# Threshold attention and a gated feed-forward block: operands laid out on the host, query tiles of two heads, float32 values in two column halves

## The chip, the cores and the metric

The program runs on one core of a Trainium2 chip. The metric is the device time of one execution in microseconds (us), lower is better. The kernel before took 1152.54 us, the median of 3 runs (1152.47 to 1153.68).

A core has a tensor engine (PE), which multiplies a stationary operand (loaded first, shown as PEld) with a moving one and writes to PSUM, and the engines DVE (vector), ACT (scalar) and POOL (GpSimd), which work on SBUF; DVE and ACT also read PSUM. SP issues the DMAs here.

## The reference, cut to what matters

```python
# q, k, v: (8 batches, 8 heads, 576 tokens, 64), float32; tau = 0.02
scores = matmul(q, k.transpose(0, 1, 3, 2)) / 8
thresh = max(scores, -1) - tau
scores = where(scores >= thresh, scores, -1e9)
attn = exp(scores - max(scores, -1))
attn = attn / (sum(attn, -1) + 1e-9)
x = matmul(attn, v)                       # then the heads side by side: (8, 576, 512)
x_prev = x one token earlier, zeros first
xk = mu_k * x + (1 - mu_k) * x_prev
xr = mu_r * x + (1 - mu_r) * x_prev
k = maximum(xk @ w_k, 0)                  # 512 -> 1024
out = sigmoid(xr @ w_r) * ((k * k) @ w_v) # 1024 -> 512
```

The weights w_k, w_r and w_v come as float64 words and are cut to float32 on the chip.

## The kernel before

**Precision.** A matmul whose operands are marked fp32r keeps fewer bits of them than float32. So most products are made of an upper part (the rounded value) and a lower part (what the rounding left): upper by upper, upper by lower, lower by upper. A matmul on plain float32 needs no split; in the trace each one is two MATMUL records with a weight load each.

**Attention.** A *job* is one batch and two heads (`hp`), 32 in all. Its 576 queries per head are cut into four tiles of 128 per head and one tile "T" that holds the last 64 queries of both heads, so nine tiles. Each tile is one *slot*, 288 in all; `full` (L633) is the order in a job. A tile goes through `scores` (L297; four matmuls of 288 columns, eight for T, through the zero-padded stationary `bd`), `row_max` (DVE, L338), `threshold` (ACT, L342), `expo` (ACT, L346), `mask` (DVE, L351), `denom` and `inverse` (DVE, L355, L358), `norm` (POOL, L361), `turn_p` (five PE transposes into `pt`, L368), `p_hi` (ACT, L393, upper part), `p_lo` (DVE, L403, lower part) and, for two tiles of a head together, `attend` (nine matmuls, L439) and `attend_out` (ACT L447, DVE L449, L456). The scores' PSUM tiles `ps_s` have two buffers, one for each of two slots.

**Operands of a job.** `load` and `load_v` fetch q, k and v with tokens on the partitions; `prep_steps` turns q and k with nine PE transposes (L189), splits them (L206 to L225), copies the parts with eight DMAs from SBUF to SBUF so that upper and lower part lie on the two halves of the partitions (`stack`, L231), fills `bd` on POOL (L249) and splits v (L277, L278). The plans `PREP` and `PREP0` (L739) spread that over the slots of the job before.

**While the tensor engine has nothing else to do.** Job 0 (`whole`) makes its scores in plain float32 (L308) on 64 partitions, and jobs 0 to 4 (`plain`) make probabilities by values in plain float32 (L412).

**Feed-forward.** 18 chunks of 256 tokens, each of 20 PE steps: eight `h` steps (twelve matmuls of 256 columns), four `z` and eight `vps` steps (six matmuls of 512 columns), all at L525. POOL and ACT mix x with x_prev and split it (L485 to L510), ACT and DVE make relu and square (L551, L554), ACT and POOL split them (L557, L558), DVE multiplies by the gate (L616), and DMAs store the rows. `weight_steps` (L119) turns one of 20 weight pieces (128 rows, 512 columns) into float32 parts, a piece every two slots: ACT (L128), DVE (L132, then L136 to L138), ACT (L142), POOL (L146). Its scratch is `xT[1]`, which later holds x of the odd batches.

**The order.** `slot(n)` (L784) issues the work of a slot, with each tile's stages spread over five slots. A credit in planned PE time decides how many feed-forward steps a slot gets: a slot adds `TSLOT` 3.325, its planned PE time is taken off, each step takes `TSTEP` 1.3, and `KEEP` 10 steps are held back until the last chunk is there. A chunk can be used from four slots after its last tile. Only ACT works strictly in this written order (L72); for the other engines a planner orders what is ready at build time, earlier lines first.

Of the kernel before, what the change touches and what calls it, by code (L numbers as in the profile page):

```python
# [15 lines left out]
# float32 readings of the upper words of the doubles 2**-127 and just under 2**128  # L16
# [5 lines left out]
def tile_threshold_attention_then_rwkv_ffn(  # L22
    ctx: ExitStack,
    tc: tile.TileContext,
    q: bass.AP,
    k: bass.AP,
    v: bass.AP,
    tau: bass.AP,
    mu_k: bass.AP,
    mu_r: bass.AP,  # L30
# [8 lines left out]
    B, H, S, D = q.shape  # L39
    DM, DF = w_k.shape  # L40
    P = 128
    NPAIR = H // 2
    NCT = DM // P
# [3 lines left out]
    NC4 = SM // P  # L47
    HS = S // 2
    KT = S
    KM = S + ST  # L50
    W = 2 * S
# [18 lines left out]
    ps_t = ctx.enter_context(tc.tile_pool(name="ps_t", bufs=1, space=bass.MemoryType.PSUM))  # L70
# [6 lines left out]
    # The threshold uses max(tau, 0).  A negative tau masks every key, which leaves  # L77
    # equal scores, so the queries are scaled by zero then.
# [9 lines left out]
    # x^T of the first 512 tokens of a batch, behind a column of what comes before  # L88
    # them (zeros), and of the last 64 tokens, behind a copy of token 511.
# [7 lines left out]
    vraw = const.tile([P, 2, 5 * D], F32, name="vraw")  # L97

    # stationaries of the scores' tile that holds both heads' last 64 queries
# [3 lines left out]
    # The weights come as float64 words.  Each is cut to float32 (saturating, with what  # L103
    # lies under float32's normal range flushed to zero): the sign and the top bit of
    # the exponent stay, the three exponent bits under it repeat it in that range, and
    # the rest moves up by three bits.
    # A piece (128 rows, 512 columns) becomes its upper and lower part, where its words lay.
    pieces = {}

    def weight_jobs():  # L110
        jobs = []
        for nm, w in (("k", w_k), ("r", w_r), ("v", w_v)):
            for f in range(w.shape[1] // 512):
                for c in range(w.shape[0] // P):
                    src = w[c * P : (c + 1) * P, f * 512 : (f + 1) * 512]
                    jobs.append(((nm, c, f), src))
        return jobs

    def weight_steps(j, key, src):  # L119
# [3 lines left out]
        w1, w0 = words[:, :, 1], words[:, :, 0]  # L123
        box = {}

        def s1():
            box["t"] = xT[1][:, j % 4 if j < 16 else 1 + (j - 16) % 3, 1 : 1 + 512]
# [23 lines left out]
    def load(job):  # L151
        b, hp = job["b"], job["hp"]
        hs = slice(2 * hp, 2 * hp + 2)
        raw = p1.tile([P, 9, 2, D], F32, tag="raw", name="raw")
        job["raw"] = raw
        for h in range(2):
            for g in range(2):
                SY.dma_start(
                    raw[:, 2 * g : 2 * g + 2, h],
                    q[b, 2 * hp + h, 2 * g * P : 2 * (g + 1) * P, :].rearrange("(p c) d -> p c d", c=2),  # L160
                )
            SY.dma_start(
                raw[:, 4:8, h], k[b, 2 * hp + h, 0:SM, :].rearrange("(p c) d -> p c d", c=NC4)
            )
        for s, src in ((0, q), (1, k)):
            SY.dma_start(
                raw[D * s : D * s + D, 8], src[b, hs, SM:S, :].rearrange("h s d -> s h d")
            )

    def load_v(job):  # L170
        b, hp = job["b"], job["hp"]
        hs = slice(2 * hp, 2 * hp + 2)
        SY.dma_start(
            vraw[:, :, 0 : 4 * D],
            v[b, hs, 0:SM, :].rearrange("h (p c) d -> p h (c d)", c=NC4),
        )
        for y in range(2):
            SY.dma_start(
                vraw[y * D : (y + 1) * D, :, 4 * D :], v[b, hs, SM:S, :].rearrange("h s d -> s h d")
            )  # L180

    def prep_steps(job):
        raw = job["raw"]
        box = {}

        def turn(nm, idx):
            ps = ps_w.tile([P, 512], F32, tag="w", name=nm)
            for j, i in enumerate(idx):
                PE.transpose(ps[:, j * P : (j + 1) * P], raw[:, i].rearrange("p h d -> p (h d)"), ident)  # L189
            box[nm] = ps  # L190

        def q_turn():
            if job["whole"]:
                job["qk"] = p3.tile([P, W], F32, tag="st1", name="qk")
                turn("pq", range(4))
                return
            box["hi"] = p1.tile([P, W], FR, tag="hi", name="hi")
            box["lo"] = p1.tile([P, W], FR, tag="lo", name="lo")
            turn("pq", range(4))

        def evac_q(cols, ps):
            if job["whole"]:
                A.activation(job["qk"][:, cols], ps, AF.Copy, scale=qscale)
                return
            hi, lo = box["hi"][:, cols], box["lo"][:, cols]
            A.activation(hi, ps, AF.Copy, scale=qscale)  # L206
            if ps.shape[1] == ST:
                tail = p2.tile([P, ST], F32, tag="tail", name="tail")
                A.activation(tail, ps, AF.Copy, scale=qscale)
                G.tensor_tensor(lo, tail, hi.bitcast(F32), op=ALU.subtract)  # L210
                return
            V.scalar_tensor_tensor(lo, ps, qscale, hi.bitcast(F32), op0=ALU.mult, op1=ALU.subtract)

        def evac_k(cols, ps):
            if job["whole"]:
                V.tensor_copy(job["qk"][:, cols], ps)
                return
            hi, lo = box["hi"][:, cols], box["lo"][:, cols]
            A.activation(hi, ps, AF.Copy)
            if ps.shape[1] == ST:  # L220
                tail = p2.tile([P, ST], F32, tag="tail", name="tail")
                A.activation(tail, ps, AF.Copy)
                G.tensor_tensor(lo, tail, hi.bitcast(F32), op=ALU.subtract)
                return
            V.tensor_tensor(lo, ps, hi.bitcast(F32), op=ALU.subtract)  # L225

        def t_evac():
            evac_q(slice(SM, S), box["pt"][:, 0:ST])
            evac_k(slice(KT, KM), box["pt"][:, ST : 2 * ST])

        def stack(h):  # L231
            if job["whole"]:
                return
            sl = slice(h * D, (h + 1) * D)
            hf, lf = box["hi"].bitcast(F32), box["lo"].bitcast(F32)
            t1 = p3.tile([P, W], FR, tag="st1", name=f"st1_{h}")
            t2 = p3.tile([P, S], FR, tag="st2", name=f"st2_{h}")
            SY.dma_start(t1[0:D].bitcast(F32), hf[sl])
            SY.dma_start(t1[D:P].bitcast(F32), lf[sl])
            SY.dma_start(t2[0:D].bitcast(F32), lf[sl, 0:S])  # L240
            SY.dma_start(t2[D:P].bitcast(F32), hf[sl, 0:S])
            job["st"][h] = (t1, t2)

        def bd_fill():
            if job["whole"]:
                return
            for h in range(2):
                for x in range(2):
                    G.tensor_scalar(  # L249
                        bd[:, 2 * h + x, h * D : (h + 1) * D],  # L250
                        job["st"][h][x][:, SM:S].bitcast(F32),
                        1.0,
                        0.0,
                        op0=ALU.mult,
                        op1=ALU.add,
                    )

        def v_split(h):
            if job["plain"]:
                if h == 0:  # L260
                    t = p3.tile([P, 5, 2, D], F32, tag="vs", name="vf")
                    for y in range(2):
                        G.tensor_scalar(
                            t[:, :, y],
# [75 lines left out]
    def threshold(x):  # L340
        nmx, thr, _, _ = x["sm"]
        A.activation(thr, nmx, AF.Identity, bias=ntau, scale=-1.0)  # L342
# [641 lines left out]
```

## Time and profile before

| | kernel before |
|---|---|
| median of 3 runs | 1152.54 us |
| span of the profiled execution | 1151.2 us |
| mean granted TensorE clock | 0.995 |
| busy us: PE, PEld | 1104.4, 999.1 |
| busy us: DVE, ACT, POOL | 961.3, 846.0, 673.3 |
| DMA moved | 105.61 MB, mean 92 GB/s |

The profiled execution's own time is its span; it lies 1.3 us under the median. A row of a group in the profile names a line of the kernel, an engine, an operation, the tiles written and read, and a count; behind the bar stand the busy time in us and the mean duration of one in ns, then the idle time before it and what ended that. A matmul's duration contains the time in which its result runs out of the array, while the next one already streams, so the distance from one start to the next is shorter than the duration; and a PE that waits inside a pipelined stretch can still be counted as busy.

### The profile page before, as it was taken

The numbers are of one execution on the slowest core, as the hardware profiler recorded it, in microseconds if no ns is written. First come the engines' busy times: TensorE is split into PE (matmuls) and PEld (weight loads), VectorE is DVE, ScalarE is ACT, GpSimd is POOL, SyncE is SP. The second block draws the span as 40 slices with busy tenths as digits, with TensorE's granted clock in tenths as the row PEclk, the third lists the DMA queues.
The fourth block names the chain that finished last, engine by engine and source line by source line (L and its number), as shares of the span: only waits on it lengthen the run. The fifth ranks groups of instructions, "written<-read, shape, count | busy, mean of one in ns | idle before, by whom it ended". The sixth has DMA issues, their size and how long they took to land.

```text
span 1151.2 us, 22514 instructions
## 1 busy us (share of the span) xinstructions
PE 1104.4 (96%) x7454; PEld 999.1 (87%) x7454; DVE 961.3 (84%) x2399; ACT 846.0 (73%) x1775; POOL 673.3 (58%) x860
## 2 busy tenths in 40 slices
PE   6999989999999999989999999999999999999998
PEld 4887878898989898988989898989898989898997
DVE  3899998888989898988989898989898989895222
ACT  3787877778687878768777878787878787876442
POOL 1465677465656465645747575656565656564672
PEclk9999999999999999999999999999999999999999
DMA  5777334433344344433334444423344444300000
GB/s 131 184 205 204 83 85 93 113 85 74 70 95 105 84 112 95 112 88 71 83 83 104 92 104 104 99 68 87 79 102 94 104 98 99 76 29 13 25 20 18
DMA packets 125027, 105.61 MB, mean 92 GB/s; under 512 B 93681, under 2 KB 101873, under 8 KB 124913
## 3 DMA queue, kind: packets, MB, share of 16 engines
q1 hardware_dynamic: 124912, 104.18, 38.8%
q8 instruction: 60, 0.98, 0.3%
q14 instruction: 55, 0.44, 0.1%
HBM read 39.85 MB, written 9.44 MB: 43 GB/s over the span
## 4 chain that ended last, share of the span: by engine, by line
PE 65%; DVE 18%; ACT 10%; issue 4%; SPq 1%; DMA 1%; POOL 1%; DVEq 0%; ACTq 0%; POOLq 0%
PE h L525 12%; PE vps L525 12%; PE pt L368 10%; PE s L326 9%; PE o L439 9%; PE z L525 8%; DVE p L351 4%; DVE sm L338 3%; DVE plo L403 2%; ACT phi L393 2%; ACT p L346 2%; DVE r L554 2%; PE o L412 1%; DVE phi L403 1%; DVE xT L137 1%
## 5 line engine op out<-in xcount | busy, mean ns | idle before, releaser
L361 POOL TENSOR_SCALAR p<-p,sm 128x576 f32<-128x576 f32 x288 | 222.6, 773 | 255.2 <-DVE sm L358 187.4
L393 ACT ACTIVATE phi<-pt 128x640 fp32r<-128x640 f32 (+1 forms) x270 | 172.4, 649 | 111.3 <-PE pt L368 110.6
L351 DVE SCALAR_TENSOR_TENSOR p<-s,sm,p 128x576 f32<-128x576 f32 x288 | 233.7, 811 | 23.4 <-ACT p L346 19.1
L338 DVE TENSOR_REDUCE sm<-s 128x1 f32<-128x576 f32 x288 | 215.9, 750 | 21.2 <-PE s L308 10.3
L525 PE MATMUL h<-xk,wk 128*128 128x256 f32 x1728 | 231.8, 285 | 1.0 <-ACT r L551 0.3
L525 PE MATMUL vps<-wv,k 128*128 128x512 f32 x864 | 227.2, 399 | 2.0 <-DVE sg L616 1.8
L368 PE MATMUL pt<-ident,p 128*128 128x128 f32 x1440 | 210.4, 276 | 18.6 <-DVE phi L403 8.9
L525 PEld LDWEIGHTS h<-xk,wk 128*128 128x128 f32 x1728 | 216.0, 191 | 4.1 <-ACT r L551 2.1
L346 ACT ACTIVATE p<-s,sm 128x576 f32<-128x576 f32 x288 | 212.6, 738 | 1.4
L368 PEld LDWEIGHTS pt<-ident,p 128*128 128x128 f32 x1440 | 168.2, 142 | 45.9 <-issue 13.5
L403 DVE TENSOR_TENSOR plo<-pt,phi 128x512 fp32r<-128x512 f32 (+1 forms) x270 | 170.5, 632 | 39.6 <-ACT phi L393 33.7
L525 PEld LDWEIGHTS vps<-wv,k 128*128 128x128 f32 x864 | 154.2, 188 | 29.1 <-DVE sg L616 2.9
L439 PE MATMUL o<-phi,vs 128*128 128x256 f32 (+1 forms) x540 | 156.1, 312 | 2.5 <-ACT phi L393 1.6
L439 PE MATMUL o<-plo,vs 128*128 128x256 f32 (+1 forms) x432 | 118.7, 296 | 0.2 <-DVE plo L403 0.2
L326 PE MATMUL s<-st 128*128 128x288 f32 x496 | 112.1, 308 | 5.0 <-DVE p L351 4.2
L558 POOL TENSOR_TENSOR k<-r,k 128x512 fp32r<-128x512 f32 x72 | 93.2, 1295 | 35.6 <-ACT k L557 35.1
L525 PE MATMUL z<-wr,xr 128*128 128x512 f32 x432 | 112.8, 400 | 0.1
L326 PE MATMUL s<-st,st 128*128 128x288 f32 x496 | 107.4, 298 | 0.1
L439 PEld LDWEIGHTS o<-phi,vs 128*128 128x128 f32 x540 | 101.8, 189 | 5.3 <-ACT phi L393 3.3
L342 ACT ACTIVATE sm<-sm,ntau 128x1 f32<-128x1 f32 x288 | 84.5, 293 | 20.8 <-DVE sm L338 19.1
L554 DVE TENSOR_TENSOR r<-r 128x512 f32<-128x512 f32 x72 | 76.8, 1066 | 27.0 <-ACT r L551 26.5
L326 PEld LDWEIGHTS s<-st 128*128 128x128 f32 x496 | 81.8, 191 | 17.4 <-DVE p L351 9.5
(91 smaller groups left out, 1792.5 us busy)
## 6 DMA issues: line engine op xcount, KB each, us to landing
st<-hi SPq DMA_DIRECT2D x62, 288.0 KB, 3.3
st<-lo SPq DMA_DIRECT2D x62, 288.0 KB, 4.1
st<-hi SPq DMA_DIRECT2D x62, 144.0 KB, 3.9
st<-lo SPq DMA_DIRECT2D x62, 144.0 KB, 4.2
raw<-in_q SPq DMA_DIRECT2D x128, 64.0 KB, 2.5
raw<-in_k SPq DMA_DIRECT2D x64, 128.0 KB, 2.9
vraw<-in_v SPq DMA_DIRECT2D x32, 256.0 KB, 2.8
out<-sg SPq DMA_DIRECT2D x32, 256.0 KB, 2.4
```

The costliest lines, as they stand in the source:

```text
L326: PE.matmul(s[:, y, 0:HS], l, r[:, KT + y * HS : KT + (y + 1) * HS], start=(j == 0), stop=(j == n - 1),)
L338: V.tensor_reduce(x["sm"][0], x["s"], axis=AX.XY, op=ALU.max, negate=True)
L346: A.activation(x["p"].rearrange("p (a b) -> p a b", a=2), x["s"], AF.Exp, bias=x["sm"][0])
L351: V.scalar_tensor_tensor(pv, x["s"], thr, pv, op0=ALU.is_ge, op1=ALU.mult, accum_out=sums)
L361: G.tensor_scalar(x["p"], x["p"], x["sm"][3], 0.0, op0=ALU.mult, op1=ALU.add)
L368: PE.transpose(x["pt"][:, c, :], x["p"][:, o : o + P], ident)
L393: A.activation(hi[:, :, off : off + sl.stop - sl.start], x["pt"][:, :, sl], AF.Copy)
L403: V.tensor_tensor(d, x["pt"][0:n, y, sl], hi[0:n, y, cs].bitcast(F32), op=ALU.subtract)
L439: PE.matmul(o[:, 0:n], l, r, start=(j == 0), stop=(j == len(prods) - 1))
L525: PE.matmul(ps, l, r, start=(x == 0), stop=(x == len(prods) - 1))
L554: V.tensor_tensor(r, r, r, op=ALU.mult)
L558: G.tensor_tensor(k2[:, 1, js], r, k2[:, 0, js].bitcast(F32), op=ALU.subtract)
```

## The change

It touches all of the attention part and the host code around it; the feed-forward chunks, their steps and the code that draws them (`micro`) stay.

- **Layout on the host.** The host passes q and k with the head dimension first, as one array `qk` of 64 rows and 1216 columns per head (q, the last 64 keys, all keys); v by pairs of heads, with the last 64 tokens of the two heads on different partitions and zeros beside them; mu as one small array; the weights' words by pieces. No arithmetic is done there.
- **Operands.** `load` fetches `qk` of one head twice, onto both halves of the partitions, into one tile `x` without a second buffer. `prep` makes, per head, the upper parts (ACT) and lower parts (DVE for q, POOL for k). The PE transposes, the SBUF-to-SBUF DMAs and the split of v are gone.
- **Slots.** A job has the tiles 0, 1, T, 2, 3; a slot holds 128 queries of both heads, or T. There are 160 slots. In batch 0 the tiles 0 and 1 of all four pairs come first, as jobs of their own, then T, 2, 3 of the four pairs. The two heads' scores take both buffers of `ps_s`.
- **Values.** The transposes of a slot (nine, six for T) go to float32 tiles `pT`, copied by ACT and DVE. `attend` multiplies float32 by float32: head 0 in the columns 0 to 63 of the array, head 1 in 64 to 127, alternating. Both groups of a job are multiplied in the slot two after its last. The jobs `plain` and `whole` are gone.
- **Rest.** `threshold` moves from ACT to DVE, the weights' `s2` from DVE to POOL; two weight pieces are begun per slot from slot 1 on; the credit has new constants.

```diff
-    TSLOT, TSTEP, KEEP, N0 = 3.325, 1.3, 10, 36
-    PLAIN, WHOLE = 5, 1
+    TPAIR, TLAST, TSTEP, KEEP = 6.85, 3.43, 1.385, 10
-    ps_t = ctx.enter_context(tc.tile_pool(name="ps_t", bufs=1, space=bass.MemoryType.PSUM))
+    ps_t = ctx.enter_context(tc.tile_pool(name="ps_t", bufs=2, space=bass.MemoryType.PSUM))
...
-            V.tensor_scalar(t, t, W_MIN, W_MAX, op0=ALU.max, op1=ALU.min)
+            G.tensor_scalar(t, t, W_MIN, W_MAX, op0=ALU.max, op1=ALU.min)
...
+    def load(job, h):
+        b, hp = job["b"], job["hp"]
+        x = p1.tile([P, W], F32, tag="x", name="x")
+        for y in range(2):
+            SY.dma_start(x[y * D : (y + 1) * D], qk[b, 2 * hp + h])
+        job["x"] = x
...
+    def prep(job, h):
...
+        A.activation(qh, x[:, 0:SM], AF.Copy, scale=qscale)
+        A.activation(kx, x[:, S:W], AF.Copy)
+        A.activation(th, x[:, SM:S], AF.Copy, scale=qscale)
+        V.scalar_tensor_tensor(
+            ql, x[:, 0:SM], qscale, qh.bitcast(F32), op0=ALU.mult, op1=ALU.subtract
+        )
+        G.tensor_tensor(kx[D:P], x[D:P, S:W], kx[D:P].bitcast(F32), op=ALU.subtract)
+        V.scalar_tensor_tensor(
+            tl, x[:, SM:S], qscale, th.bitcast(F32), op0=ALU.mult, op1=ALU.subtract
+        )
...
+    def scores(x):
...
+        if t == "T":
+            sets = [[(bd[:, 2 * h + y], h) for h in range(2) for y in range(2)]]
+        else:
+            cs = slice(t * P, (t + 1) * P)
+            sets = [[(job[w][:, h, cs], h) for w in ("qh", "ql")] for h in range(2)]
+        for u, prods in enumerate(sets):
+            o = 0 if u else ST
+            s = ps_s.tile([P, 2, 512], F32, tag="s", name="s")
...
+    def turn(x, g):
+        job, t, p = x["job"], x["t"], x["p"]
+        ps = ps_t.tile([P, 512], F32, tag="pt", name="pt")
...
+    def evac(x, g, e):
...
+            copy(e, pT[:, 3 * g : 3 * g + 3, o : o + P], ps[:, 0:384].rearrange("p (c q) -> p c q", q=P))
...
+    def attend(job, g):
+        n = 256 + g * ST
+        pT, vt = job["pT"][g], job["v"]
+        o = ps_w.tile([P, 512], F32, tag="w", name="o")
+        for c in range(5):
+            for h in range(2):
+                hs = slice(h * D, (h + 1) * D)
+                i = 4 if c == 4 else 5 * h + c
+                PE.matmul(o[hs, 0:n], vt[:, c, hs], pT[:, i], start=(c == 0), stop=(c == 4))
+        return o
+
+    def attend_out(job, g, o):
+        b, hp = job["b"], job["hp"]
+        A.activation(xT[b % 2][:, hp, 1 + g * 256 : 1 + (g + 1) * 256], o[:, 0:256], AF.Copy)
+        if g:
+            A.activation(xE[:, hp, b % NE, 1 : 1 + ST], o[:, 256 : 256 + ST], AF.Copy)
...
+        if b == 0:
+            for tiles in ([0, 1], ["T", 2, 3]):
+                for hp in range(NPAIR):
+                    add(b, hp, tiles)
+        else:
+            for hp in range(NPAIR):
+                add(b, hp, [0, 1, "T", 2, 3])
...
+        n = job["due"] = job["last"] + 2
+        av_at[n] = [(job, g) for g in job["groups"]]
...
+        def tensor_time():
+            pe = 0.0
+            if x is not None:
+                pe += 1.05
+            if x1 is not None:
+                pe += 0.56 if x1["t"] == "T" else 0.98
+            for _, g in avs:
+                pe += 10 * (256 + g * ST) * 2 / 2400 + 0.2
...
+        if x is not None:
+            scores(x)
+        flush_a()
+        if x is not None:
+            row_max(x)
+            threshold(x)
+        av(0)
+        one_step()
+        if x1 is not None:
+            turn(x1, 0)
+            turn(x1, 1)
+        if x is not None:
+            expo(x, 0)
+        if x1 is not None:
+            evac(x1, 0, A)
+        if x is not None and x["n"] > 1:
+            expo(x, 1)
+        if x1 is not None:
+            evac(x1, 1, V)
+            if x1["t"] != "T":
+                turn(x1, 2)
+                evac(x1, 2, A)
+        av(1)
+        if x is not None:
+            mask(x)
+            inverse(x)
+            norm(x)
+        rest()
+        one_step()
...
+        if chunks and chunks[0]["first"]:
+            if len(chunks[0]["mix"]) > 7:
+                chunks[0]["mix"].pop(0)()
+        for c in ready.get(n, []):
+            chunks.append(ffn_chunk(*c))
+        while state["credit"] > 0 and micro(keep):
+            state["credit"] -= TSTEP
+        state["credit"] = min(state["credit"], 0.0)
+        for _ in range(2):
             for w in list(wq):
                 w.pop(0)()
                 if not w:
                     wq.remove(w)
+            if wjobs and n >= 1:
+                j = 20 - len(wjobs)
+                wq.append([lambda: None] + weight_steps(j, *wjobs.pop(0)))
```

More of the change, by code (lines that the diff above doesn't have):

```diff
@@ L298, in scores @@
         job, t = x["job"], x["t"]
[L299 to L306 removed]
+        x["s"] = []
+        if t == "T":
[3 more added lines that the diff above has]
+            sets = [[(job[w][:, h, cs], h) for w in ("qh", "ql")] for h in range(2)]
@@ L370, in group @@
-    def group(job, h, g):
-        if (h, g) not in job["groups"]:
-            job["groups"][(h, g)] = (
-                p2.tile([P, 5, 320], FR, tag="phi", name="phi"),
-                p2.tile([P, 4, 320], FR, tag="plo", name="plo"),
-            )
-        return job["groups"][(h, g)]
-    def dests(x):
-        job, t = x["job"], x["t"]
-        if t[0] == "T":
-            return [
-                (group(job, h, job["tg"]), 2 * P, slice(h * ST, (h + 1) * ST)) for h in range(2)
-            ]
-        h, c = t
-        return [(group(job, h, c // 2), (c % 2) * P, slice(0, P))]
@@ new lines, in scores, with row_max @@
+                        s[:, y, 0:HS],
+                        l,
+                        job["kx"][:, h, o + y * HS : o + (y + 1) * HS],
+                        start=(j == 0),
+                        stop=(j == len(prods) - 1),
+                    )
+            x["s"].append(s[:, :, 0:HS])
+        x["n"] = len(sets)
+        x["sm"] = p3.tile([P, 8], F32, tag="sm", name="sm", bufs=6)
+        x["p"] = p3.tile([P, 2, S], F32, tag="p", name="p")
+    def row_max(x):
+        sm = x["sm"]
+        for u in range(x["n"]):
+            V.tensor_reduce(sm[:, u : u + 1], x["s"][u], axis=AX.XY, op=ALU.max, negate=True)
@@ new lines, in threshold, with halves, expo, mask @@
+    def threshold(x):
+        sm = x["sm"]
+        for u in range(x["n"]):
+            V.tensor_scalar(
+                sm[:, 2 + u : 3 + u], sm[:, u : u + 1], -1.0, ntau, op0=ALU.mult, op1=ALU.add
+            )
+    def halves(ap):
+        return ap.rearrange("p (a b) -> p a b", a=2)
+    def expo(x, u):
+        A.activation(halves(x["p"][:, u]), x["s"][u], AF.Exp, bias=x["sm"][:, u : u + 1])
+    def mask(x):
+        sm = x["sm"]
+        for u in range(x["n"]):
+            pv = halves(x["p"][:, u])
+            V.scalar_tensor_tensor(
+                pv,
+                x["s"][u],
+                sm[:, 2 + u : 3 + u],
+                pv,
+                op0=ALU.is_ge,
+                op1=ALU.mult,
+                accum_out=sm[:, 4 + u : 5 + u],
+            )
@@ new lines, in inverse, with norm, group @@
+    def inverse(x):
+        sm, n = x["sm"], x["n"]
+        V.tensor_scalar(sm[:, 4 : 4 + n], sm[:, 4 : 4 + n], 1e-9, None, op0=ALU.add)
+        V.reciprocal(sm[:, 6 : 6 + n], sm[:, 4 : 4 + n])
+    def norm(x):
+        for u in range(x["n"]):
+            p = x["p"][:, u]
+            G.tensor_scalar(p, p, x["sm"][:, 6 + u : 7 + u], 0.0, op0=ALU.mult, op1=ALU.add)
+    def group(job, g):
+        if g not in job["pT"]:
+            job["pT"][g] = p1.tile([P, 9, 256 + g * ST], F32, tag=f"pT{g}", name=f"pT{g}")
+        return job["pT"][g]
@@ L656, in tile_threshold_attention_then_rwkv_ffn @@
-    av_at = {}
-    for (ji, h, g), n in last_slot.items():
-        if not jobs[ji]["plain"]:
-            av_at.setdefault(n + 4, []).append((ji, h, g))
-    ready = {}
-    def when(sel):
-        return max(n for (ji, h, g), n in last_slot.items() if sel(jobs[ji], g)) + 4
+        job["last"] = len(slots) - 1
+    av_at, ready, edge_at = {}, {}, {}
+    for ji, job in enumerate(jobs):
+        n = job["due"] = job["last"] + 2
+        av_at[n] = [(job, g) for g in job["groups"]]
     for b in range(B):
@@ L680, in tile_threshold_attention_then_rwkv_ffn @@
+    prep_at = {}
+    for ji, job in enumerate(jobs[:-1]):
+        off = {2: 0, 3: 1, 5: 2}[len(job["tiles"])]
+        for h in range(2):
+            prep_at[job["start"] + off + h] = (ji + 1, h)
     wjobs = weight_jobs()
@@ L835, in one_step, with av @@
+        state["credit"] -= tensor_time()
+        def one_step():
+            if state["credit"] > 0 and micro(keep):
                 state["credit"] -= TSTEP
-        def more_steps():
-            while state["credit"] > 0 and micro(keep):
-                state["credit"] -= TSTEP
-            state["credit"] = min(state["credit"], 0.0)
+        def av(k):
+            if k < len(avs):
+                job, g = avs[k]
+                attend_out(job, g, attend(job, g))
         def rest():
@@ new lines, in slot @@
+        av(1)
+        if x is not None:
+            mask(x)
[3 more added lines that the diff above has]
+        one_step()
+        if n in prep_at:
+            ji, h = prep_at[n]
+            prep(jobs[ji], h)
+            if h == 0:
+                load(jobs[ji], 1)
+                load_v(jobs[ji])
+            elif ji + 1 < len(jobs):
+                load(jobs[ji + 1], 0)
+        if n in edge_at:
+            b = edge_at[n]
+            G.tensor_scalar(
+                xE[:, :, b % NE, 0:1],
+                xT[b % 2][:, :, SM : SM + 1],
+                1.0,
+                0.0,
+                op0=ALU.mult,
+                op1=ALU.add,
+            )
```

563 lines of the change are left out of this document (98 added, 465 removed).

## The prediction

> **What bounds the kernel now.** I read first the page's busy times, then the busy times by stage, then the chain of waits for the price of each step.
>
> ```profile
> PE 1104.4 (96%) x7454; PEld 999.1 (87%) x7454; DVE 961.3 (84%) x2399; ACT 846.0 (73%) x1775; POOL 673.3 (58%) x860
> ```
>
> ```profile
> L525 PE MATMUL h<-xk,wk x1728: 274/283/388, 162.4 to 1130.0; 128*128 128x256 f32 x192
> ```
>
> ```profile
> 30.00:162.40 132.40, 121.47 (x845) 105.14 (x845) 123.10 (x288) 106.06 (x242) 77.83 (x98) 0.97 0.63 163
> 162.40:1060.00 897.60, 876.35 (x6038) 803.10 (x6037) 807.86 (x2061) 695.11 (x1450) 539.76 (x691) 1.00 0.38 87
> 1060.00:1151.00 91.00, 86.65 (x519) 77.33 (x517) 19.10 (x21) 34.84 (x63) 49.44 (x55) 1.00 0.07 21
> ```
>
> The columns of the windows are the stretch, its length, then busy us of PE, PEld, DVE, ACT, POOL. The reader is to see three stages. Until 162.4 us there is no feed-forward work, and DVE is busy 123.1 of 132.4 us, 93%: DVE sets the pace. From 162.4 to 1060 PE is the bound, and at the end PE works off feed-forward steps alone.
>
> A busy PE is not PE at its peak, so I price its work by the steps of the chain of waits, which don't overlap (start, us, what):
>
> ```profile
> 523.55 1.38 PE vps L525 x6
> ...
> 527.38 1.31 PE o L439 x9
> ...
> 539.74 1.06 PE s L326 x8
> ...
> 548.33 0.55 PE pt L368 x5
> 548.88 1.07 PE o L439 x9
> ...
> 550.48 1.44 PE h L525 x12
> ```
>
> So a vps or z matmul costs 0.23 us, an h 0.12, a score 0.1325, a transpose 0.11, a value matmul 0.119 or 0.146 (mean 0.133). The groups of PE between 162.4 and 1060 us count how many there are:
>
> ```profile
> L525 PE MATMUL h<-xk,wk 128*128 128x256 f32 x1440 | 196.7, 286 | 1.0 <-ACT r L551 0.3
> L525 PE MATMUL vps<-wv,k 128*128 128x512 f32 x708 | 191.1, 401 | 2.0 <-DVE sg L616 1.8
> L368 PE MATMUL pt<-ident,p 128*128 128x128 f32 x1225 | 175.5, 274 | 12.7 <-DVE phi L403 8.9 <-POOL bd L249 1.0 <-POOL p L361 0.8
> L439 PE MATMUL o<-phi,vs 128*128 128x256 f32 (+1 forms) x539 | 155.8, 312 | 2.5 <-ACT phi L393 1.6 <-DVE sg L616 0.9
> L439 PE MATMUL o<-plo,vs 128*128 128x256 f32 (+1 forms) x432 | 118.7, 296 | 0.2 <-DVE plo L403 0.2
> L525 PE MATMUL z<-wr,xr 128*128 128x512 f32 x360 | 95.9, 401 | 0.1
> L326 PE MATMUL s<-st 128*128 128x288 f32 x428 | 93.6, 300 | 0.7 <-DVE p L351 0.2
> L326 PE MATMUL s<-st,st 128*128 128x288 f32 x430 | 92.8, 297 | 0.0
> L326 PE MATMUL s<-st,bd 128*128 128x288 f32 x216 | 34.5, 299 | 1.5 <-DVE p L351 1.5
> ```
>
> 1440 x 0.12 + 1068 x 0.23 + 1225 x 0.11 + 971 x 0.133 + 1074 x 0.1325 = 172.8 + 245.6 + 134.8 + 129.1 + 142.3; the 260 matmuls left (mostly the turning of q and k) at 0.11 add 28.6. That is 853 of 897.6 us: PE stalls for about 44 us, 4.9%.
>
> **The change, part by part: PE.** Feed-forward is untouched: a chunk is 8 x 1.44 + 12 x 1.38 = 28.1 us, a step 1.404, all 360 steps 505 us. The q and k transposes go (9 x 0.11 per pair, 32 us in all). Scores stay at 40 matmuls per pair: 5.30 us. Transposes fall from 45 to 42: 4.62 us. What is new is the value product in float32 with one head in each column half. The nearest rows are the float32 scores of job 0, whose tile T has two heads in separate quarters of the array:
>
> ```profile
> 27.86 2.63 PE L412 MATMUL o<-pf,vf 128*128 128x128 f32 x10
> 30.43 1.62 PE L308 MATMUL s<-qk 64*64 64x288 f32 x8
> ...
> 32.58 1.47 PE L412 MATMUL o<-pf,vf 128*128 128x128 f32 x10
> 33.89 1.13 PE L308 MATMUL s<-qk 64*128 64x288 f32 x4
> 34.95 0.33 PE L368 MATMUL pt<-ident,p 128*128 128x128 f32 x1
> ```
>
> ```profile
> 31.40 0.14 PEld L308 LDWEIGHTS s<-qk 64*64 64x64 f32 x2 [0.20 <-issue]
> ```
>
> ```profile
> L308 PE MATMUL s<-qk x40: 402/684/846, 10.3 to 40.1; 64*128 64x288 f32 x32, 64*64 64x288 f32 x8
> ```
>
> The same ten records take 2.63 us at 27.86 and 1.47 us at 32.58, so the array ran at about half speed before 31.4. At full speed four full-width records of 288 columns start (1.13 - 0.402)/3 = 0.243 us apart; eight in a row would take 7 x 0.243 + 0.402 = 2.10. The eight quarter records took 1.62, half of them still at half speed, and their weight loads come in twos: the two heads ran side by side, a pair for the price of one. By columns a pair costs 0.216 us for 256 and 0.270 for 320 (estimates from 0.243). One group is 10 pairs, and the array changes its split before and after: at 33.89 the fourth record starts at 34.62, its 0.243 end at 34.86, and the next starts at 34.95, 0.09 late; 0.19 for both. So 2.35 + 2.89 = 5.24 us per pair of heads. If nothing overlapped it would be 2 x 4.86 + 0.38 = 10.1. I take 5.24, since the row shows the overlap, though for quarters with rows of their own.
>
> The Trainium skill, "TensorE: Matmul & The Clock Gate", Part 3 ("What overlaps and what doesn't"), has a rule against this: a weight load overlaps running matmuls only when their row groups differ, and the two halves share all rows. By it each pair would show a load, and the sum would be the 1255 of the last rival. The trace disagrees for the full array: an h matmul of one row group follows another every 0.12 us although
>
> ```profile
> L525 PEld LDWEIGHTS h<-xk,wk 128*128 128x128 f32 x1728 | 216.0, 191 | 4.1 <-ACT r L551 2.1 <-DVE lo L212 0.7 <-DVE sm L355 0.3
> ```
>
> its load alone lasts 0.191; no run here shows it for column halves.
>
> Attention is then 5.30 + 4.62 + 5.24 = 15.16 us of PE per pair of heads.
>
> **The start.** Feed-forward begins when eleven mixing steps of the first chunk are issued, one per slot from slot 10 on: at the end of slot 20, with batch 0 through. Until then DVE counts, as before:
>
> ```profile
> L351 DVE SCALAR_TENSOR_TENSOR p<-s,sm,p 128x576 f32<-128x576 f32 x288 | 233.7, 811 | 23.4 <-ACT p L346 19.1
> ...
> L338 DVE TENSOR_REDUCE sm<-s 128x1 f32<-128x576 f32 x288 | 215.9, 750 | 21.2 <-PE s L308 10.3 <-PE s L326 8.9
> ...
> L554 DVE TENSOR_TENSOR r<-r 128x512 f32<-128x512 f32 x72 | 76.8, 1066 | 27.0 <-ACT r L551 26.5
> ...
> L358 DVE RECIPROCAL sm<-sm 128x1 f32<-128x1 f32 x288 | 45.6, 158 | 5.1
> ...
> L351 DVE DVE_READ_ACCUMULATOR p<-s,sm,p 128x1 f32 x288 | 23.5, 82 | 0.0
> L212 DVE SCALAR_TENSOR_TENSOR lo<-pq,qscale,hi 128x512 fp32r<-128x512 f32 x31 | 23.2, 748 | 0.9 <-ACT hi L206 0.2
> ...
> L216 DVE COPY qk<-pk 128x512 f32<-128x512 f32 x1 | 0.7, 692 | 4.8 <-PE pk L189 4.8
> ```
>
> and the whole DVE time of the weights' lines 136, 137 and 138, in this order (stretch, length, busy us):
>
> ```profile
> 0.00:1151.20 1151.20, 12.77 (x20) 1.00 0.39 92
> ...
> 0.00:1151.20 1151.20, 20.82 (x20) 1.00 0.39 92
> ...
> 0.00:1151.20 1151.20, 18.70 (x20) 1.00 0.39 92
> ```
>
> A pair slot costs 2 x (0.750 + 0.811 + 0.082) + 4 x 0.158 (thresholds, now here, one sum, one reciprocal) = 3.92 us, a T slot 2.12. The copy of 384 transposed columns is 0.55, T's three copies 0.8 (estimates from 0.692 for 512). The lower part of q is 0.95 per head with its tail; its nearest rows are 0.748 from PSUM and 1.066 with both operands in SBUF, so up to 1.3. The weights cost 52.3, the same as before less `s2`. Slots 0 to 20 are 17 pair slots and 4 T: 66.6 + 8.5 + 12 (copies) + 17 (18 heads, since batch 0 makes its operands twice) + 52.3 = 156 us. At the 93% of before that is 168 us. The first score started at 10.3 before; now the key's lower part on POOL stands ahead of it too, so I put 12. **Feed-forward starts at 180 us**, 18 later than before. The load of `x` has one buffer, so each head's load waits for the parts of the head before. The nearest DMA,
>
> ```profile
> st<-hi SPq DMA_DIRECT2D x62, 288.0 KB, 3.3
> ```
>
> makes some 7 us per head with the parts, under the 8 to 11 us of a slot with weights. I cost it at nothing; DVE's weight work covers it, and without that cover (slots 0 to 3) it is up to 10 us.
>
> **After it.** Of the 160 slots, the rest holds 28 pairs: 424 us less slot 20's 2. Steps: a pair earns 4 x 6.85 + 3.43 = 30.8 of credit, 9.7 + 5.2 of planned time go off, and 15.9 / 1.385 = 11.5 steps are drawn, while 11.25 come in. They come in lots (40 a batch, 60 with an "end" chunk) two slots after a batch's last, and ten are kept. Counted slot by slot, 290 steps are drawn by slot 160, 70 stay for the end, and slots 33 to 40 and 59, 60, 79, 80 have one or none. PE work until slot 161: 422 + 290 x 1.404 = **830 us**. Stalls: 4.9% of it would be 41; the waits of transposes on the split (`pt <- DVE phi` 8.9 of 12.7 in its row) go, others come (below), so I take 4%, **33**. The empty slots go at DVE's pace: 37 us for slots 33 to 40 (7 x 4.47 + 2.9 + 3 x 0.95) against 23 of PE work, and some 7 for the other four; the planner can draw a few steps forward: **18**. The end: 70 x 1.404 = **98**, and the last window's idle 4.4.
>
> Sum: 180 + 830 + 33 + 18 + 98 + 4.4 = 1163.4 us of span. The span of before lies 1.3 under the median, so **1165 us**, 1.1% slower. In short: a tile is cheaper for PE, but the float32 products that filled the idle PE early are gone and the start is longer.
>
> **Costed at nothing.** POOL loses the split of v and `bd`, and gains the key's lower part and `s2`; ACT loses the threshold, and makes q and k parts for each head twice over. Both stay under 80% of PE by the page's shares, and PE covers them after slot 20; DVE's weights do before. If ACT were late, `evac` would be, and behind it the third transpose, which needs one of two `ps_t` buffers. On SP, eight SBUF-to-SBUF DMAs per pair go. DVE in the steady stretch has some 26 us per pair against 31 of PE.
>
> **The rivals.**
>
> *Fewer stalls (faster).* PE no longer needs a split between transposes and values. If stalls in slots 21 to 161 fall to 1% (8 us) and steps drawn forward fill all but 5 us of the empty slots, the time is 1165 - 25 - 13 = 1127. It decides from 15 us saved. For it: DVE falls from 90% (807.9 of 897.6) to 84%. Against: shorter distance between scores and masks.
>
> *Scores wait for masks (slower).* Both buffers of `ps_s` now belong to one slot, so a slot's scores wait for the masks of the slot before, and behind them on PE stand transposes, values and steps in order. Before, with one buffer to spare:
>
> ```profile
> PE s L326 <- DVE p L351: 5.7, 9, 2.2
> ```
>
> At 0.4 us in each of 111 pair slots it gives 1165 + 44 = 1209.
>
> *The halves don't overlap.* 32 x 4.86 = 155 more: 1320. The change would not do what it says.
>
> *Weight loads of the halves show.* Each of 20 record pairs per pair of heads would add the 0.14 of the load row at 31.40: 2.8 x 32 = 90, so 1255. This is what the Trainium skill's rule, named above, would do.
>
> **How the numbers follow.** Forecast 0.50, its own range 1140 to 1195; fewer stalls 0.28; scores wait 0.13; no overlap 0.05; loads show 0.04. A change under 0.2% (2.3 us) can't be told from none. The forecast's own range holds 0.08 faster and 0.06 within; with the 0.28, faster is 0.36, same 0.06, slower 0.58. The range 1113 to 1213 takes in the faster case down to 14 us below its 1127 (a start at 166, if DVE's early stalls vanish) and the waiting case up to 4 above its 1209; it leaves out the last two cases (0.09) and the tails of the others, under 0.2 in all.
>
> **What would show it.** The first h step near 180 us, with DVE over 90% before it; value records that start in twos and 2.35 and 2.89 us per group; 70 steps after the last values; gaps of PE at slots 33 to 40. It is wrong if the first h comes before 160, if value records follow one by one, or if PE waits for masks in most slots.

## The result, and the profile after

The kernel after takes 1346.96 us (median of 4 runs, 1345.43 to 1349.56), the kernel before, run beside it, 1152.51 (1151.62 to 1153.68): a ratio of 1.170, 95% interval 1.167 to 1.173. Slower was forecast, but by 1%, and 1347 lies far outside the range of 1113 to 1213.

The page of the kernel after, its busy times and the chain that ended last:

```profile
PE 1153.5 (86%) x6928; PEld 894.7 (67%) x6928; DVE 901.5 (67%) x2013; ACT 730.0 (54%) x1436; POOL 735.5 (55%) x702
...
PE 46%; DVE 17%; POOL 11%; ACT 10%; DMA 10%; issue 4%; SPq 1%; POOLq 0%; ACTq 0%; DVEq 0%
PE o L305 13%; DMA x<-in_qk 10%; PE s L197 8%; PE pt L270 7%; PE h L379 7%; PE vps L379 7%; DVE sm L212 4%; PE z L379 4%; POOL p L249 4%; DVE bd L177 3%; ACT p L225 3%; DVE p L231 2%; POOL kx L176 2%; DVE ql L173 2%; ACT qh L170 2%
```

DVE and ACT are busy for fewer us than before. PE is busy for 49 us more although it has fewer matmuls, and it is idle for 1343.3 - 1153.5 = 190 us against 47. No engine is the bound; they wait for each other, and less than half of the chain is PE's. A transfer, the load of `x`, holds 10% of it.

By stage (stretch, length, busy us of PE, PEld, DVE, ACT, POOL, granted clock, DMA share, GB/s):

```profile
50.00:100.00 50.00, 28.41 (x108) 17.14 (x108) 40.65 (x76) 21.11 (x40) 37.82 (x27) 0.59 0.46 136
100.00:150.00 50.00, 26.46 (x95) 16.86 (x95) 41.41 (x72) 25.25 (x49) 44.42 (x30) 0.55 0.23 57
150.00:200.00 50.00, 31.79 (x132) 20.40 (x130) 37.73 (x80) 21.93 (x47) 30.61 (x25) 0.64 0.21 53
...
600.00:800.00 200.00, 182.73 (x1137) 143.26 (x1136) 144.67 (x336) 115.48 (x234) 108.25 (x109) 0.97 0.21 55
...
1250.00:1300.00 50.00, 50.00 (x313) 45.32 (x312) 11.74 (x12) 21.86 (x43) 34.66 (x33) 1.00 0.06 22
```

From 50 to 200 us DVE is busy 120 of 150 us, 80% and not the 93% of before, and the clock that PE is granted averages 0.55 to 0.64. In the middle PE is busy 91%; the last window is feed-forward alone, as before.

Three stages can be cut at the first `h` and at the last value matmul. The rows of the groups (count, ns least/median/most, first and last start, tiles) for the kernel after:

```profile
L379 PE MATMUL h<-xk,wk x1728: 274/283/416, 208.8 to 1322.0; 128*128 128x256 f32 x192
...
L305 PE MATMUL o<-pT,v x1280: 379/432/797, 38.5 to 1240.8; 128*64 128x256 f32 x93, 128*64 128x320 f32 x90
```

| stage, us | forecast | after |
|---|---|---|
| to the first `h` | 180 | 208.8 |
| to the last value matmul | 881 | 1032.0 |
| to the end of the span | 102.4 | 102.5 |
| span | 1163.4 | 1343.3 |

The end is right to 0.1 us. Of the 180 us that are missing, 29 lie in the start and 151 in the middle. The waits of the kernel after give the candidates (who waited, for whom: us, times, longest):

```profile
ACT xT L310 <- PE o L305: 130.3, 56, 6.6
ACT qh L170 <- DMA x<-in_qk: 110.7, 38, 7.1
...
POOL p L249 <- ACT qh L170: 53.1, 14, 6.3
...
PE pt L270 <- POOL p L249: 44.9, 41, 2.5
PE s L197 <- DVE p L231: 42.8, 32, 6.7
...
PE pt L270 <- DVE pT L277: 32.9, 28, 3.2
```

**Theory 1, the load.** `x` has one buffer, so a head's load is issued only when the last part of the head before is made, and ACT, which works in its written order, stands at L170 until it lands. Behind ACT stand the exponentials, the masks, the scores. One such place in the middle, from the chain of waits (start, us, what):

```profile
640.66 1.52 DVE bd L177
...
642.23 0.47 SPq L154
...
642.75 4.50 DMA x<-in_qk
...
647.26 0.03 ACT qh L170
```

and from the timelines of ACT, DVE and PE (start, us, engine, line; in brackets the idle time before it and its releaser):

```profile
647.26 0.72 ACT L170 ACTIVATE qh<-x,qscale 128x512 fp32r<-128x512 f32 x1 [2.34 <-DMA x<-in_qk]
...
652.20 0.72 ACT L225 ACTIVATE p<-s,sm 128x576 f32<-128x576 f32 x1
...
652.96 0.82 DVE L231 SCALAR_TENSOR_TENSOR p<-s,sm,p 128x576 f32<-128x576 f32 x1 [1.33 <-ACT p L225]
...
653.84 0.53 PE L197 MATMUL s<-kx,qh 128*128 128x288 f32 x2 [1.63 <-DVE p L231]
```

`bd` ends at 642.18, the load goes out and takes 4.5 us, ACT resumes at 647.26 and makes its parts of `x`. Before its next exponential, at 652.20, it waits 2.33 us more, for a square of the feed-forward on DVE (L408), which comes there behind DVE's own parts of the same `x`. The mask follows at 652.96, and PE has waited 1.63 us when it starts the scores at 653.84.

**Rivals.** *Depth*: the transposes stand one slot behind the scores and wait for POOL's norm and for the copies; the kernel before spread a tile's stages over five slots. *POOL's clamp*: `s2`, for which I gave POOL no price, takes 2.08 us there, and from 100 to 150 us POOL is busy 44.4 of 50 us. The same operation in the groups of the kernel after, on POOL, and in those of the kernel before, on DVE:

```profile
L128 POOL TENSOR_SCALAR xT<-xT 128x512 f32<-128x512 f32 x20 | 41.6, 2079 | 0.2
```

```profile
L132 DVE TENSOR_SCALAR xT<-xT 128x512 f32<-128x512 f32 x20 | 9.4, 470 | 0.0
```

*Copies of values on ACT*: they stand ahead of the exponentials in the written order, and wait 130.3 us for the value matmuls. *DMA bandwidth*: each head is fetched twice.

### The profile page after: what moved, and what is told of

It is laid out like the page before. It is cut to its first block, busy times and chain, and to the rows that moved or that the text cites. A ratio compares the mean times of both kernels' runs of the same rounds, so it can differ in the third digit from the quotient of the medians.

```text
span 1343.3 us, 19614 instructions
## 1 busy us (share of the span) xinstructions
PE 1153.5 (86%) x6928; PEld 894.7 (67%) x6928; DVE 901.5 (67%) x2013; ACT 730.0 (54%) x1436; POOL 735.5 (55%) x702
## 4 chain that ended last, share of the span: by engine, by line
PE 46%; DVE 17%; POOL 11%; ACT 10%; DMA 10%; issue 4%; SPq 1%; POOLq 0%; ACTq 0%; DVEq 0%
PE o L305 13%; DMA x<-in_qk 10%; PE s L197 8%; PE pt L270 7%; PE h L379 7%; PE vps L379 7%; DVE sm L212 4%; PE z L379 4%; POOL p L249 4%; DVE bd L177 3%; ACT p L225 3%; DVE p L231 2%; POOL kx L176 2%; DVE ql L173 2%; ACT qh L170 2%
## 5 line engine op out<-in xcount | busy, mean ns | idle before, releaser
L270 PE MATMUL pt<-ident,p 128*128 128x128 f32 (+1 forms) x1344 | 232.6, 301 | 94.4 <-POOL p L249 44.9
L270 PEld LDWEIGHTS pt<-ident,p 128*128 128x128 f32 (+1 forms) x1344 | 159.5, 149 | 176.7 <-POOL p L249 80.4
L305 PE MATMUL o<-pT,v 128*64 128x256 f32 (+1 forms) x1280 | 217.6, 438 | 4.7 <-ACT pT L275 4.5
L275 ACT ACTIVATE pT<-pt 128x384 f32<-128x384 f32 (+3 forms) x352 | 149.7, 428 | 125.4 <-PE pt L270 85.5
L197 PE MATMUL s<-kx,qh 128*128 128x288 f32 x512 | 132.3, 340 | 57.5 <-DVE p L231 34.1
L176 POOL TENSOR_TENSOR kx<-x,kx 64x640 fp32r<-64x640 f32 x72 | 119.1, 1654 | 99.8 <-ACT kx L171 78.1
L277 DVE COPY pT<-pt 128x384 f32<-128x384 f32 (+3 forms) x224 | 94.9, 430 | 92.7 <-PE pt L270 86.6
L305 PEld LDWEIGHTS o<-pT,v 128*64 128x64 f32 x1280 | 97.9, 144 | 80.3 <-issue 28.2
L197 PEld LDWEIGHTS s<-kx,qh 128*128 128x128 f32 x512 | 90.4, 209 | 90.2 <-DVE p L231 29.5
L197 PE MATMUL s<-kx,ql 128*128 128x288 f32 x512 | 120.6, 320 | 0.0
L170 ACT ACTIVATE qh<-x,qscale 128x512 fp32r<-128x512 f32 x72 | 51.8, 720 | 110.7 <-DMA x<-in_qk 110.7
L408 DVE TENSOR_TENSOR r<-r 128x512 f32<-128x512 f32 x72 | 76.8, 1066 | 32.8 <-ACT r L405 32.3
```

Of the source, the lines that this page charges most:

```text
L176: G.tensor_tensor(kx[D:P], x[D:P, S:W], kx[D:P].bitcast(F32), op=ALU.subtract)
L197: PE.matmul(s[:, y, 0:HS], l, job["kx"][:, h, o + y * HS : o + (y + 1) * HS], start=(j == 0), stop=(j == len(prods) - 1),)
L270: PE.transpose(ps[0:m, j * P : (j + 1) * P], blocks[i], ident)
L275: A.activation(d, s, AF.Copy)
L277: e.tensor_copy(d, s)
L305: PE.matmul(o[hs, 0:n], vt[:, c, hs], pT[:, i], start=(c == 0), stop=(c == 4))
```

## The experiments

Each variant has one run. They come in three groups, each on one chip with the kernel before beside it, which took 1154.6 us with the first four, 1149.9 with the next four and 1153.9 with the last three. So a difference of less than some 5 us between two groups says nothing. The kernel after, to which the first four and the depth alone are compared, ran from 1345.4 to 1349.6.

### A second buffer for x

```diff
-        x = p1.tile([P, W], F32, tag="x", name="x")
+        x = p2.tile([P, W], F32, tag="x", name="x")
...
-        job["v"] = p2.tile([P, 5, P], F32, tag="v", name="v")
+        job["v"] = p1.tile([P, 5, P], F32, tag="v", name="v")
...
+        if avs:
+            nj = [j for j in jobs if j["start"] == avs[0][0]["last"] + 1]
+            for j in nj:
+                load_v(j)
...
-                load_v(jobs[ji])
```

To make room, `v` gives up its second buffer and is loaded after the values that read it.

> The tile x gets a second buffer; to make room, v has one buffer and is fetched after the values of the job before. Load theory (ScalarE, in its written order, waits 110.7 us for the DMA of x, and exponentials, masks and scores stand behind it): the waits of qh for x fall under 20 us and the time falls by 60 us or more, to 1285 or less. Weights theory (POOL's clamp of the weights at 2.1 us a piece holds the first 160 us): at most 15 us faster, and the first 160 us stay as they are. Values-copy theory (ScalarE waits 130 us for the value matmuls in front of the exponentials): at most 30 us faster.

Measured: **1279.4**, 68 less, as the load theory had it. The row `ACT qh <- DMA x` is gone from its waits. The first `h` comes at 185.7 us for 208.8, 23 earlier, and the stretch from there to the last value matmul takes 989.4 us for 1032.0, 43 less.

### No loads of x after the first

```diff
+    x_one = const.tile([P, W], F32, name="x_one")
+    x_all = [x_one, x_one]
...
-        x = p1.tile([P, W], F32, tag="x", name="x")
+        x = x_all[h]
...
-            SY.dma_start(x[y * D : (y + 1) * D], qk[b, 2 * hp + h])
+            if job is jobs[0] and h == 0:
+                SY.dma_start(x[y * D : (y + 1) * D], qk[b, 2 * hp + h])
```

> x is fetched once, for the first head of the first job, and all heads use it; the other 71 fetches are left out, all the work on x stays, the output is that of one head's q and k everywhere. Load theory: at least as fast as with two buffers, 1285 or less. Weights theory: 15 us at most, with POOL still full from 50 to 160 us. If the masked sums differ in no way that costs time, the kernel is otherwise the same.

Measured: **1276.4**, 71 less. Its middle moved 18 GB/s where that of the second buffer moved 54 (750 us of each, columns as above):

```profile
300.00:1050.00 750.00, 705.27 (x4486) 554.89 (x4485) 540.63 (x1296) 459.21 (x899) 422.75 (x417) 0.98 0.20 54
```

```profile
300.00:1050.00 750.00, 707.16 (x4496) 556.18 (x4497) 541.34 (x1296) 461.14 (x903) 424.91 (x417) 0.98 0.06 18
```

Without the traffic 3 us more are gained, so it was the wait, not the bytes; and since `load_v` stays where it was here, its move in the experiment before is not what made the difference. The load is the largest of the causes tried, but with two buffers 125 us over the kernel before remain.

### The clamp back on DVE

```diff
-            G.tensor_scalar(t, t, W_MIN, W_MAX, op0=ALU.max, op1=ALU.min)
+            V.tensor_scalar(t, t, W_MIN, W_MAX, op0=ALU.max, op1=ALU.min)
```

> Only the clamp of the weights goes back to DVE. Weights theory: POOL is no longer full from 50 to 160 us, slot 20 starts 30 to 40 us earlier than 219, and the time falls to about 1310. Load theory: the slots then wait for x instead, at most 10 us faster. Values-copy theory: no change beyond 10 us.

Measured: **1337.1**, 10 less, where the theory of the clamp had about 1310.

### The copies of values behind the exponentials

```diff
-        av(0)
+        o0 = attend(*avs[0]) if avs else None
...
+        if avs:
+            attend_out(*avs[0], o0)
```

> The copy of the first group's values to xT is written after the exponentials of its slot, the second group's copy stays. Values-copy theory: the wait of ScalarE for the value matmuls falls from 130 us to under 70 and the time falls by 40 us or more. Load theory and weights theory: less than 15 us, since the wait moves to the next thing that is late.

Measured: **1342.2**, 5 less, little more than the kernel after varies by itself. The wait of ACT for the value matmuls fell as that theory had it, from 130.3 to 64.5 us, and the time did not follow. The theory of the copies falls.

### Transposes and values one slot later

The edit, first on top of the second buffer, then alone:

```diff
-        n = job["due"] = job["last"] + 2
+        n = job["due"] = job["last"] + 3
...
-            x1 = slots[n - 1] if 0 <= n - 1 < NS else None
+            x1 = slots[n - 2] if 0 <= n - 2 < NS else None
...
-    for n in range(NS + 3):
+    for n in range(NS + 4):
```

> The two buffers of x of the first experiment, and the transposes of a tile two slots behind its scores in place of one (the values then three slots behind the job's last). With two buffers the tensor engine still took 34.7 us per pair of heads against 31.3 of priced work, and most of the excess stood in front of transposes. Depth theory (a tile is transposed in the slot right after its scores, so the chain maximum, exponential, mask, normalisation ends just too late): 31.5 to 33 us per pair, 1225 or less. Copy theory (the excess is the wait for the copies out of the two transposes' buffers and the changes of the array's split around the values, both of which stay): at least 34 us per pair, 1260 or more.

> The depth without the second buffer of x. If the load chain is a limit of its own, ScalarE still waits for x behind its written order and little is won: 1320 or more. If depth alone hides it, 1290 or less.

Measured: **1241.3** with the second buffer, 38 less than that alone; **1306.4** alone, 41 less than the kernel after. The two gains add up (68 + 41 = 109 against 106 together), so these are two causes and not one seen twice. Each result lies between its two forecasts, so the depth was worth less than its theory had it (1225 or less), and it neither hides the load (1290 or less) nor is hidden by it (1320 or more). What PE waited for between 300 and 1050 us, first with the second buffer alone:

```profile
PE pt L270 <- POOL p L249: 15.3, 19, 2.0
PE pt L270 <- ACT pT L275: 13.9, 7, 3.6
...
PE s L197 <- DVE p L231: 1.1, 3, 0.5
```

then with the depth as well:

```profile
PE s L197 <- DVE p L231: 11.5, 20, 1.4
PE pt L270 <- DVE pT L277: 9.4, 10, 1.1
PE pt L270 <- ACT pT L275: 8.0, 13, 1.3
```

Between 300 and 1050 us the wait for POOL's norm goes altogether. Some of it comes back as the wait of scores for masks, in short pieces.

### The clamp again, on top

The edit of the clamp with the second buffer, and with both:

> Two buffers of x, and the clamp of the weights on DVE. With two buffers POOL was busy 97% from 50 to 150 us and DVE 92%. Weights theory: the clamp alone won 10 us while x was late; now that x is not, it should win 15 to 25, 1255 to 1265. If DVE is the limit by then (the forecast's own count), it wins under 8.

> Two buffers, depth and clamp together. If the three causes are separate their gains add to those of the two-buffer kernel: by the depth theory and the weights theory about 1210. If they hide one another, 1240 or more.

Measured: **1284.3**, 5 more than the second buffer alone in the other group, and **1240.9**, 0.4 less than both without it. With the clamp on DVE, DVE is full where it wasn't (the first with second buffer and depth, the second with the clamp too):

```profile
50.00:100.00 50.00, 24.05 (x108) 15.44 (x108) 42.53 (x75) 23.15 (x44) 48.13 (x32) 0.72 0.55 156
```

```profile
50.00:100.00 50.00, 24.75 (x108) 15.62 (x108) 49.89 (x85) 23.93 (x44) 31.46 (x23) 0.64 0.50 145
```

POOL falls from 48.1 to 31.5 us, DVE rises from 42.5 to 49.9, and the time stays: the work changes hands. The forecasts for a cause of its own, 1255 to 1265 and about 1210, both fail: the clamp's place is worth 10 us in the kernel after and nothing once the other two are mended.

### Head 0's five chunks, then head 1's

On top of the second buffer and the depth:

```diff
-            for c in range(5):
-                for h in range(2):
+            for h in range(2):
+                for c in range(5):
```

> On the kernel with two buffers and depth (1241), the values of a group in another order: the five chunks of head 0, then the five of head 1, in place of turn and turn about. If the two column halves overlap only for neighbours in the order, as the starts in twos suggest, a group of 256 takes 4.5 us in place of 2.4 and the time rises by up to 150 us, to 1340 to 1390 (the end, with feed-forward alone, hides nothing of it). If the halves never overlapped, or if the array looks far ahead, the time stays within 10 us of 1241.

Measured: **1315.5**, 74 more. The same 20 records, in the written order of two heads by turns, and then head by head:

```profile
651.29 2.38 PE L305 MATMUL o<-pT,v 128*64 128x256 f32 x20
```

```profile
651.35 3.73 PE L305 MATMUL o<-pT,v 128*64 128x256 f32 x20
```

By turns the group takes 2.38 us, where 2.35 was forecast. Head by head it takes 3.73, against 20 x 0.216 + 0.19 = 4.5 if nothing overlapped. So the halves do run side by side, and the written order is what gives most of it. The starts of the 20 records in the second trace show what is left of the overlap: the first six come one by one, about 0.22 us apart, the next eight overlap, and the last six come one by one again, as if the second head's first records ran beside the first head's last ones. The forecast for this order, 1340 to 1390, had no such overlap.

### One weight piece a slot, and copies moved from DVE

On top of the second buffer and the depth; the second run has the last line as well:

```diff
-        for _ in range(2):
+        for y in range(2):
...
-            if wjobs and n >= 1:
+            if wjobs and n >= 1 and y == 0:
...
-            evac(x1, 1, V)
+            evac(x1, 1, A if n < 20 else V)
```

> On the same kernel, one weight piece begun per slot in place of two, over slots 1 to 20. DVE and POOL were over 90% busy from 50 to 150 us and about 79% and 60% from 150 to 200. If the start is DVE's sum (the forecast's count), evening it out wins at most 10 us, 1231 to 1241. If the start is set by ScalarE's written order, which waits for each weight piece on DVE in front of the exponentials, fewer such waits per slot win 15 to 25.

> As the one before, and in slots 0 to 19 DVE's copies of the transposes go to ScalarE, which was half idle there: 11 us of DVE's sum. If the start is DVE's sum, 8 to 11 us less than the one before; if it is ScalarE's order, no better or worse.

Measured: **1231.4**, 10 less than with two pieces, or 14 when each is taken against the kernel before in its own group, and **1244.1**, 13 more than that. The first result lies at the edge of what DVE's sum would give and short of what ACT's order would. The second goes against the sum. The first 170 us of the one (one piece a slot), then of the other:

```profile
0.00:170.00 170.00, 105.11 (x476) 68.69 (x476) 146.89 (x306) 92.14 (x185) 124.53 (x99) 0.78 0.53 149
```

```profile
0.00:170.00 170.00, 101.04 (x428) 67.49 (x428) 134.04 (x268) 91.75 (x183) 113.67 (x92) 0.77 0.50 142
```

With less work on DVE, DVE is not full (134 of 170 us) and still less gets done, PE's records too (428 for 476). ACT has only 92 us of work there. What PE waited for in these 170 us, first with one piece a slot, then with the copies moved as well:

```profile
PE pt L270 <- DVE pT L277: 17.2, 10, 4.1
...
PE s L197 <- DVE p L231: 10.5, 8, 2.1
PE pt L270 <- ACT pT L275: 9.4, 8, 2.7
```

```profile
PE pt L270 <- ACT pT L275: 20.1, 12, 4.0
PE s L197 <- DVE p L231: 19.9, 12, 2.9
...
PE pt L270 <- DVE pT L277: 6.5, 3, 3.2
```

The wait for DVE's copies shrinks by 10.7 us, but the wait for ACT's copies grows by as much, and the masks come later, for 9.4 us more. That fits copies that moved into a queue which is worked off strictly in its written order. ACT's waits for weight pieces that DVE has not finished are not what tells the two apart: they are longer in the faster run (`wk` alone 23.1 us against 19.0).

## Why the prediction was wrong

The forecast lacked 182 us (1347 against 1165). Two of its terms are shown to have failed, and together they hold 106 to 109 us of that; with both mended the kernel still takes 1241, 76 over the forecast.

**The load of `x`, costed at nothing.** This is the step that failed, and the costliest of those shown. I had the load (some 7 us per head with its parts) and the single buffer, and compared that with the slot's length. But it isn't a slot's length that matters, it is who stands still meanwhile: ACT, in its written order, with the exponentials of the slot behind it. The cover that I named, DVE's weight work, is gone after slot 20, while the load comes twice per pair of heads to the end. Measured: 68 us, 23 of them in the start and 43 in the middle.

**Stalls of 4%, 33 us.** I carried the 4.9% of before over, and made it less because transposes no longer wait for a split. But they wait for something else: POOL's norm is now one slot ahead at most, and the float32 copies take the place of the split. Moving transposes and values a slot back gave 38 to 41 us, more than the whole term. I listed "scores wait for masks" as a rival with 44 us, and the kernel after shows 42.8 us of that wait; but with a second buffer for `x` it falls to 14.3 over the whole run, though `ps_s` still has its two buffers:

```profile
PE s L197 <- DVE p L231: 14.3, 16, 2.0
```

So most of it came with the late exponentials and not from the buffers. With the depth as well it is 23.6.

**The start at 180.** It came at 208.8, since the load stood in the way there too. With the second buffer it is 185.7, with the depth as well 182.0, with one piece a slot 161.2:

```profile
L379 PE MATMUL h<-xk,wk x1728: 274/283/562, 185.7 to 1256.3; 128*128 128x256 f32 x192
```

```profile
L379 PE MATMUL h<-xk,wk x1728: 274/283/506, 182.0 to 1218.3; 128*128 128x256 f32 x192
...
L305 PE MATMUL o<-pT,v x1280: 379/432/797, 32.8 to 1133.6; 128*64 128x256 f32 x92, 128*64 128x320 f32 x91
```

```profile
L379 PE MATMUL h<-xk,wk x1728: 274/283/562, 161.2 to 1208.3; 128*128 128x256 f32 x192
...
L305 PE MATMUL o<-pT,v x1280: 379/432/796, 32.2 to 1123.7; 128*64 128x256 f32 x92, 128*64 128x320 f32 x91
```

So 180 was about the start of a kernel without that wait, but partly by luck: by DVE's sum the run with moved copies should have started earlier than the one without, at 161.2, and it started at 173.5.

**What was right.** The end: 70 steps, 102.5 us. The price of the halves, and with it the fall of two rivals: a 256-wide group takes 2.38 us. The weight loads don't show: one lasts 0.144 us in the row

```profile
L305 PEld LDWEIGHTS o<-pT,v 128*64 128x64 f32 x1280 | 97.9, 144 | 80.3 <-issue 28.2 <-ACT pT L275 6.1 <-ACT r L405 1.3
```

and ten pairs with their two changes of split fit into 2.38, less than 0.24 each. If no load overlapped a matmul, a pair would take at least 0.216 + 0.144 = 0.36, by estimate from these rows. The rule of the Trainium skill, "TensorE: Matmul & The Clock Gate", Part 3 ("What overlaps and what doesn't"), that a load overlaps matmuls only of other row groups, is contradicted here, since a load of 128 rows shares them all with the matmuls beside it. That POOL and ACT have room was also right as a sum over the span, and useless: ACT was held by its order, and POOL had little room early, where the clamp stood.

The 320-wide group did not get the price forecast for it. The planner lets a group of transposes in between: 1.29 us for 6 records, the transposes, then 2.37 for 14 (at 654.40 in the run with the second buffer and the depth), together 3.66 against 2.89. In the records' starts the last two before the cut and the last two of the group come alone, without a partner in the other half.

**What stays open.** The best version, 1231, starts feed-forward at 161.2 us, the kernel before at 162.4, and yet it is 77 us slower than that one beside it. Of the 21 us that one piece a slot won at the start, 11 are lost again behind it. Its middle (161.2 to 1123.7) is 962.5 us instead of 881, with nearly the attention work that was forecast for it (1120 score, 1194 transpose and 1140 value records). The forecast's priced work there is 830, so its stalls and empty slots, put at 33 + 18 = 51, come to some 132 even here. Its PE waits between 300 and 1050 us name no large one:

```profile
PE s L197 <- DVE p L231: 11.8, 21, 1.4
PE pt L270 <- DVE pT L277: 9.0, 9, 1.1
PE pt L270 <- ACT pT L275: 6.9, 12, 1.3
PE s L197 <- DVE pT L277: 6.7, 7, 1.1
```

If I price the records between 250 and 1100 us by the prediction's steps, some 115 of 850 us are left over, where the same count left 44 of 897.6 in the kernel before: 29 at changes of split into and out of the values, 24 where transposes follow feed-forward (13 of it comes back behind them), 24 where scores do, 16 inside groups of transposes, and some 35 in smaller pieces. Where scores follow feed-forward, most places leave nothing and a quarter leave much, and in the kernel before all such places together left under 2 us from 250 to 1050; so these look like late masks and not like a price of the change itself. Changes of split are more than forecast in number, by the cut above. Which of these pieces is cause and which only follows was not tried.

## What to carry to other kernels

A load into a single buffer is priced by the engine that stands at it and by all that its written order holds behind it, not by whether the sum fits into a slot. When a change shortens the distance between stages, the stalls of before are no estimate for after: list each pair of neighbours with the slots between them, and ask which producer is late first. Sums of busy time bound nothing where every engine has room; there the order decides, and moving work off the fullest engine can make it slower, as the copies moved to ACT did.

## What the runs showed of the hardware that I had not expected

- Two column halves overlap by turns, 2.38 us for 20 records, and much less head by head, 3.73.
- The same two-limit clamp of 128 x 512 float32 takes 2.08 us on POOL and 0.47 on DVE.
- A PE that was busy 53 to 64% was granted a clock of 0.55 to 0.64 (50 to 200 us of the kernel after), and work done there takes longer: a group of 14 value records took 3.35 us at 204.89 in the kernel after, with a granted clock of 0.71 from 204 to 209 us, where the same count took 2.37 at a clock of 1.00 with the second buffer and the depth. The mean granted clock of the span rose from 0.928 to 0.965 between these two kernels. So a part of what the waits cost comes as a slower clock.

```profile
204.89 3.35 PE L305 MATMUL o<-pT,v 128*64 128x320 f32 x14
```

```profile
656.10 2.37 PE L305 MATMUL o<-pT,v 128*64 128x320 f32 x14
```
